# Softmax of the first two sub-blocks with one token per partition: dynamic convolution and squared-ReLU FFN

## The chip, the cores and the metric

The kernel runs on one core of a Trainium2 chip. The metric is device time in microseconds (us) of one execution; lower is better. The engines are PE (matmul, with its weight loads shown apart as PEld), DVE (vector), ACT (scalar), POOL (GpSimd) and SP (which here only issues DMAs). ACT and POOL can issue DMAs too.

## What is computed

The reference, cut to what matters (B=8, S=4096, D=192, 8 heads of 24 channels, K=7 taps, 2048 hidden columns):

```python
w = exp(weight_gen - max)                     # (B, S, 8 heads, 7 taps)
w = w / sum(w, axis=-1)                       # softmax over the taps
x_unf = x_pad[:, s + k, :]                    # 6 zeros ahead of x
out = einsum('bshk,bskhg->bshg', w, x_unf)    # a causal 7-tap conv, its weights differ by token and head
h = maximum(out.reshape(-1, 192) @ w_in, 0)   # w_in 192 x 2048
result = (h * h) @ w_out                      # w_out 2048 x 192
```

## The kernel before, in words

**Tiling.** The 32768 tokens are cut into 64 sub-blocks of 512 tokens (TB). The first two sub-blocks are blocks of their own, the others go in pairs; the FFN runs over blocks. For the conv a sub-block is cut into five row tiles (NT=5) of 128 tokens, placed 104 apart from 24 tokens before its start (`starts`), so that each tile holds the 6 tokens before the ones it yields. For every row tile the conv needs a banded matrix: row = input token, column = output token and head, value = the softmax weight of that tap.

**How the band is made.** A `Softmax` part covers 128*r tokens with r tokens per partition: load of the weights (`load`, L219), exp on ACT (L244), sum over the taps on DVE (L251), reciprocal (L258), and scaled products written along diagonals (L266) into a tile v, in which a token's row holds 8 shifted places for the weights. The rows must then get from "r tokens per partition" to "one token per partition in row tile i": the tile `wr`. For most parts this is a DMA (`wr_load`, or `wr_load_sbuf` at L361, which reads v in SBUF). For the first two sub-blocks it is done by PE: `select_rows` (L383) multiplies v by slices of a 0/1 matrix `sel`, 8 matmuls of 64 columns a row tile, and `copy_rows` (L391, ACT) brings the PSUM result to `wr`. `st_band` (L406, DVE) then multiplies `wr` by a band mask into `bd`.

**The conv and the FFN.** `st_conv_first` (L466) multiplies x in f16 by `bd`, 16 small matmuls a row tile, into PSUM; the result is copied to y (L476 on ACT and L477 on DVE for sub-block 0, L479 for sub-block 1). A unit of the FFN (`st_unit`) is a set of matmuls of y by w_in (L566 for the first two blocks, L581 later), Relu on ACT (L595) and a square on DVE (L599). The second matmul (L630) multiplies by w_out, and o_sb (L644, L646) collects the output.

**Order.** All instructions are written in a fixed order, engine by engine, by a plan string per block: `u` a unit, `B` bands, `C` the next conv, `E` an exp, `S` the rest of a softmax, `M` a second matmul, `L` a load. Engines run their instructions in that order; DMA queues are those of SP, POOL and ACT. The first FFN unit follows a written prologue:

- PE runs 46 matmuls on zeros (`spin`, L697).
- SP issues the loads of the first part s0 (14 rows a partition, in three pieces: 8 tokens and a halo of 6), x of sub-block 0 in f32 (`x_st`, L317 and L327), and half of w_in in f32 (`w_st`, L133 and L135).
- s0 has r=8, so it covers 1024 tokens: sub-blocks 0 and 1.
- POOL makes the band mask (L117, L120) and `sel` (L110), then waits for s0's reciprocal through a one-element copy (`gate`, L716), then issues x of sub-block 1, the other half of w_in (in f16, the DMA casts) and the weights of the next part s1. A second gate (L746) waits for `w_st`; then follow w_out (L183), s2's weights and x of sub-block 2.
- ACT casts x_st to f16 in three pieces (L342) between the copies of the selected rows: tile 0; copies of tiles 0 and 1; tiles 1 and 2 of x; copies of tiles 2 to 4; tiles 3 and 4 of x.
- ACT casts one half of w_st (columns of units 0 and 1; L740) ahead of the copy of y, DVE the other half (units 2 and 3) after it.

Of the kernel before, what the change touches and what calls it, by code (L numbers as in the profile page):

```python
# [9 lines left out]
def kernel(  # L10
# [26 lines left out]
    nc = tc.nc  # L37
    f32 = mybir.dt.float32
    f16 = mybir.dt.float16

    B, S, D = x.shape
# [3 lines left out]
    HK = H * KK  # L45
# [3 lines left out]
    HP = H // 2  # L49
# [47 lines left out]
    w_o = const.tile([P, NF, Dm], f16, name="w_o")  # L97
    mask = const.tile([P, P, 2], f16, name="mask")
    FIRST = 8
    NSEL = TB + TB - P + FIRST + P  # L100
    sel = const.tile([P, NSEL], f16, name="sel")
    PARTS = {0: (8, 8, 8, 8), 1: (8, 8, 16), 2: (16, 16)}
    v_big = const.tile([P, R + 2 * HALO, HP, SL, 2], f16, name="v_big")
    v_first = [
        const.tile([P, FIRST + 2 * HALO, HP, SL, 2], f16, name=f"v_first{i}") for i in (0, 1)
# [1 line left out]

    def row_select():

        nc.gpsimd.affine_select(  # L110
            out=sel, in_=sel, pattern=[[-1, NSEL]], compare_op=AluOp.not_equal,
            fill=1.0, base=FIRST - 1, channel_multiplier=FIRST,
        )

    def band_mask():
# [11 lines left out]


    x_st = {}

    def load_w_in(dst, q, eng):
        c = q * NQ
# [58 lines left out]
    class Softmax:  # L191
# [86 lines left out]
        def store(self, eng):  # L278
# [5 lines left out]
                in_=self.v[:, HALO : HALO + r].rearrange("p r g c e -> p (r g c e)"),  # L284
            )

    vd_t = {}

    def new_vd(b):
# [2 lines left out]
        return vd_t[b]  # L292


    x_t, wr_t, pr_t, bd_t, yp_t, y_t, g_t, gp_t, t1_t, o_t, o_sb_t = ({} for _ in range(11))

    def rows(ap2d, t0, width):

# [4 lines left out]

    def ends(b):
        rs = PARTS.get(b, (R,))
        return [P * sum(rs[: i + 1]) for i in range(len(rs))]

    def tile_start(j, i):

# [42 lines left out]
    def wr_load_sbuf(j, parts, order, engines):  # L352

        wr_t[j] = p_wr.tile([P, NT, HP, SL * 2], f16, name="wr")
        n = 0
        for i in order:
            t0 = max(j % NBB * TB + tile_start(j, i), 0)
            for s in parts:
                a, b = max(t0, s.t0), min(t0 + P, s.t0 + P * s.r)
                if a < b:  # L360
                    engines[n % len(engines)].dma_start(  # L361
                        out=wr_t[j][a - t0 : b - t0, i].rearrange("p g c -> p (g c)"),
                        in_=s.v[
                            (a - s.t0) // s.r : (b - s.t0) // s.r, HALO : HALO + s.r
                        ].rearrange("p r g c e -> p r (g c e)"),
                    )
                    n += 1

    def select_rows(j, s, tiles, places):

        if j not in wr_t:
            wr_t[j] = p_wr.tile([P, NT, HP, SL * 2], f16, name="wr")
        n = len(tiles) // len(places)
        for m, i in enumerate(tiles):
            if m % n == 0:
                pool, tag = places[m // n]
                prs = pool.tile([P, n, H * SL], f32, name="pr", tag=tag)
                pr_t[(j, i)] = prs
            pr = prs[:, m % n]
            a = max(j % NBB * TB + tile_start(j, i), 0) - s.t0  # L380
            for r in range(s.r):
                c = a + FIRST - 1 - r
                nc.tensor.matmul(  # L383
                    out=pr, lhsT=sel[:, c : c + P],
                    rhs=s.v[:, HALO + r].rearrange("p g c e -> p (g c e)"),
                    start=(r == 0), stop=(r == s.r - 1),
                )

    def copy_rows(j, tiles, n=1):
        for i in tiles[::n]:  # L390
            nc.scalar.copy(  # L391
                out=wr_t[j][:, i : i + n].rearrange("p t g c -> p t (g c)"),
                in_=pr_t.pop((j, i)),
            )

    def st_band(j, tiles):

# [48 lines left out]
    def st_conv_first(j):  # L446

        s = BLOCKS[j][0]
        y = p_y.tile([P, NK, TB], f16, name="y")
        y_t[j] = y  # L450
        if j == 0:
            yps = [ps_h.tile([P, TB], f32, name="yp", tag="h") for _ in range(2)]
        else:
            yp = ps_h.tile([P, 2, TB], f32, name="yp", tag="h")
            yps = [yp[:, k] for k in (0, 1)]
        places = [(q, 32 * q, 0) for q in range(4)]
        places += [(q, r0 + 32 * (q - 4), 1) for r0 in (0, RT) for q in (4, 5)]
        for i in ROW_ORDER:
            lo, b = bounds[i], bounds[i + 1]
            hi = lo + (STEP if tile_start(s, i) == starts[i] else b - lo)  # L460
            bd = bd_t[s][:, H * lo : H * hi].rearrange("p (g c e) -> p g e c", g=HP, e=2)
            for later in (True, False):
                for q, p0, k in places:
                    _, ha, hb, pre = quads[q]
                    m, h = (32, hb) if later else (pre, ha)
                    nc.tensor.matmul(  # L466
                        out=yps[k][p0 : p0 + m, lo:b],
                        lhsT=x_t[s][:, i, 32 * q : 32 * q + m],
                        rhs=bd[:, h // 2, h % 2, 0 : b - lo],
                        start=True,  # L470
                        stop=True,
                        skip_group_check=True,
                        tile_position=(0, p0),
                    )
        if j == 0:
            nc.scalar.copy(out=y[:, 0], in_=yps[0])  # L476
            nc.vector.tensor_copy(out=y[:, 1], in_=yps[1])  # L477
        else:
            nc.scalar.copy(out=y[:, 0:2], in_=yp)  # L479

    def st_conv_spread(j):

# [183 lines left out]
    with nc.allow_low_precision("fp16 matmul pipeline"), tc.manual_schedule():  # L666

        block_of = {n: j for j, (s, c) in enumerate(BLOCKS) for n in range(s, s + c)}
        parts = []
        for b in range(B):  # L670
            t0 = 0
            for r in PARTS.get(b, (R,)):
                v = v_first[len(parts) % 2] if r == FIRST else v_big
                parts.append(Softmax(b, t0, r, v, block_of[b * NBB + t0 // TB]))
                t0 += P * r
# [7 lines left out]
                wr_load_sbuf(j, near, range(NT), engines)  # L683

        warm = const.tile([P, TB], f16, name="warm")
        gate = const.tile([P, 1], f32, name="gate")
        nc.vector.memset(warm, 0.0)
        nc.vector.memset(sel, 0.0)
        for v in v_first:
            nc.vector.memset(v[:, HALO : HALO + FIRST], 0.0)  # L690

        WARM = 156
        wp = ps_o.tile([P, TB], f32, name="wp", tag="o0")
# [5 lines left out]
                    start=True, stop=True,  # L699
                )  # L700

        s0, s1, s2 = parts[:3]
        spin(46)
        band_mask()
        s0_cuts = (0, FIRST // 2, FIRST, s0.rh)
        s0.load(nc.sync, s0_cuts)
        w_st = p_wg.tile([P, (R + HALO) * HK], f32, name="w_st", tag="wg")[:, 0 : NQ + NQ // 2]
        x_load_f32(0)
        row_select()
        load_w_in(w_st, 0, nc.sync)  # L710
        for lo, hi in zip(s0_cuts, s0_cuts[1:]):
            s0.exp(lo, hi)
            s0.total(lo, hi)
            if hi >= FIRST:
                s0.recip(0 if hi == FIRST else FIRST, hi)
        nc.gpsimd.tensor_copy(out=gate, in_=s0.rcp[:, FIRST, 0, 0:1])  # L716
        x_load(1)
        load_w_in(w_i[:, 1, 0], 1, nc.gpsimd)
        s1.load(nc.gpsimd)
        s0.scale(0, s0.rh, nc.vector)  # L720
        x_cast(0, nc.scalar.copy, 0, 1)
        o0, o1, ring = (ps_o, "o0"), (ps_o, "o1"), (ps_h, "h")
        select_rows(0, s0, ROW_ORDER, (o1, ring, ring, ring, o0))
        copy_rows(0, ROW_ORDER[:2])
        x_cast(0, nc.scalar.copy, 1, 3)
        copy_rows(0, ROW_ORDER[2:])
        x_cast(0, nc.scalar.copy, 3, NT)
        for i in ROW_ORDER:
            st_band(0, (i,))
        select_rows(1, s0, ROW_ORDER, (o1,))  # L730
        copy_rows(1, ROW_ORDER, NT)

        def cast_w_in(e, copy):

            q = NQ // 4
            w0, w1 = (
                w.rearrange("p (a e c) -> p a e c", e=2, c=q)[:, :, e]
                for w in (w_st, w_i[:, 0, 0])
            )
            copy(out=w1, in_=w0)  # L740

        cast_w_in(0, nc.scalar.copy)
        st_conv_first(0)
        cast_w_in(1, nc.vector.tensor_copy)

        nc.gpsimd.tensor_copy(out=gate, in_=w_st[:, 0:1])  # L746
        for q in range(4):
            load_w_out(q, 4)
        s2.load(nc.gpsimd)
        x_load(2)  # L750
# [5 lines left out]
        steady = "MuMuuu" * 3 + "MuuuMCu"  # L756
        steady_spread = "MuMuuu" * 2 + "MuCMuuu" + "MuMuuu"
        plans = {
            0: "u B1 u u u E1 C S1 u u M u u",
            1: "L3 u u B2 M E2 B3 u u M E2 u S2 S2 u M u C u M",  # L760
            2: "L4 u u u E3 M u u u M B4 u u u u M B5 S3 u u u u M u C u",
            3: "L5 L6 u u E3 u M S3 u u u M u M E4 u u B6 u M u M B7 u u u E4 M u M C S4 u",
        }


# [23 lines left out]

        for n, s in enumerate(parts):  # L790
            k = n - min(m for m, p in enumerate(parts) if p.b == s.b)
            cuts = (0, s.rh) if n < 2 else CUTS_FOR.get((s.b, k), CUTS[s.r])
            s.pieces = list(zip(cuts, cuts[1:]))
            s.exps = iter(s.pieces)
            s.softs = iter(s.pieces)
        for n, s in enumerate(parts[4:], 4):
            b, f = s.b, s.fb
            k = n - min(m for m, p in enumerate(parts) if p.b == b)
            times = TIMES.get((b, k)) or (
# [156 lines left out]
```

## Time and profile before

| What | Value |
|---|---|
| runs | 729.57, 729.58, 731.94 us; median 729.58 us |
| the profiled execution: span from the first to the last instruction | 728.4 us |
| PE busy | 722.0 us (99%), 14078 matmuls |
| DVE busy | 625.8 us (86%) |
| ACT busy | 612.0 us (84%) |
| POOL busy | 98.5 us (14%) |
| granted TensorE clock | 1.000 |
| DMA | 68.30 MB, mean 94 GB/s |

The profiled execution's device time is not recorded apart from its span; what lies around the span is taken from the median of the runs, 729.58 - 728.4 = 1.2 us. The profile is of one execution. Its lines give, for an engine, a start and a length in us from the first instruction; "[0.80 <-DMA wg]" means that the engine had been idle for 0.80 us and that this load ended it. "L266" is line 266 of the kernel. "128x224 f32" is partitions by elements. The chain is followed back from the last instruction, at each step to what released it.

### The profile page before, as it was taken

To read this page: it belongs to the slowest core of one execution; us is meant where nothing else is said; L and a number is where in the kernel's file an instruction comes from. 1 tells how busy PE (TensorE), PEld (TensorE's weight loads), DVE (VectorE), ACT (ScalarE), POOL (GpSimd) and SP (SyncE) were. 2 spreads that over 40 slices of the span, in tenths; PEclk is the share of its full clock that TensorE was granted. 3 is DMA by queue.
4 is the path that set the end of the run, shared out by engine and by line. 5 is a ranking of instruction groups with operands and counts; after the bars stand their busy time and mean duration, and the time that the engine had idled before them with its cause. 6 is when DMAs were issued, how large, how long until landed. Compare 5 with 4: busy or idle time off the path is not lost.

```text
span 728.4 us, 31046 instructions
## 1 busy us (share of the span) xinstructions
PE 722.0 (99%) x14078; PEld 530.1 (73%) x14078; DVE 625.8 (86%) x839; ACT 612.0 (84%) x731; POOL 98.5 (14%) x146
## 2 busy tenths in 40 slices
PE   8999999999999999999999999999999999999998
PEld 5668877777777777777777777777777777777777
DVE  7999997998898998888988888988888988778753
ACT  6998888888888888888888888888888888888883
POOL 7231223411001100011001010010000110001000
PEclk9999999999999999999999999999999999999999
DMA  9664465676245443356432554343544325444112
GB/s 193 128 113 106 82 125 89 128 142 138 78 71 133 99 84 68 75 116 125 83 62 58 135 104 88 66 74 110 114 78 87 57 53 117 67 87 77 30 46 67
DMA packets 126272, 68.30 MB, mean 94 GB/s; under 512 B 85353, under 2 KB 122556, under 8 KB 125628
## 3 DMA queue, kind: packets, MB, share of 16 engines
q0 software_dynamic: 46192, 19.43, 22.9%
q1 hardware_dynamic: 79804, 46.79, 22.5%
q8 instruction: 110, 1.80, 1.1%
q14 instruction: 22, 0.18, 0.1%
q10 hardware_dynamic: 144, 0.10, 0.0%
HBM read 50.18 MB, written 28.70 MB: 108 GB/s over the span
## 4 chain that ended last, share of the span: by engine, by line
PE 98%; DMA 1%; SPq 0%; ACT 0%; issue 0%; ACTq 0%
PE o L630 47%; PE h L581 44%; PE yp L502 4%; PE h L566 2%; PE yp L536 1%; DMA w_st<-in_moe_w_in_dram 1%; SPq L219 0%; PE yp L466 0%; ACT w_i L740 0%; SPq L135 0%; SPq L133 0%; ACT y L476 0%; SPq L327 0%; SPq L317 0%; ACT o_sb L644 0%
## 5 line engine op out<-in xcount | busy, mean ns | idle before, releaser
L595 ACT ACTIVATE t<-h 128x1024 f16<-128x1024 f32 x512 | 496.6, 1027 | 60.1 <-PE h L581 58.4
L630 PEld LDWEIGHTS <-g 64*128 64x128 f16 (+1 forms) x8032 | 344.3, 94 | 55.2 <-issue 2.3
L630 PE MATMUL o<-w_o,g 64*128 64x192 f16 (+1 forms) x8032 | 380.1, 243 | 0.1
L599 DVE TENSOR_TENSOR g<-t 128x2048 f16<-128x2048 f16 (+1 forms) x287 | 307.4, 1105 | 28.7 <-ACT t L595 28.3
L581 PE MATMUL h<-y,w_p 64*128 64x512 f16 x2400 | 291.7, 376 | 0.0
L581 PEld LDWEIGHTS <-w_p 64*128 64x128 f16 x2400 | 113.9, 94 | 94.8
L406 DVE TENSOR_TENSOR bd<-wr,mask 128x4160 f16<-128x4160 f16 (+4 forms) x90 | 149.5, 1685 | 1.2 <-ACT wr L391 1.2
L646 DVE TENSOR_TENSOR o_sb<-o,o_sb 128x384 f32<-128x384 f32 x123 | 68.4, 556 | 61.4 <-ACT o_sb L644 60.3
L327 POOL DMA_DIRECT2D xt<-in_x_dram x63 | 52.6, 838 | 415.4 <-PE yp L502 362.5
L644 ACT COPY o_sb<-o 128x384 f32<-128x384 f32 x129 | 61.6, 477 | 45.7 <-PE o L630 44.4
L581 PE MATMUL h<-y,w_i 64*128 64x512 f16 x576 | 70.5, 376 | 0.0
L581 PEld LDWEIGHTS <-w_i 64*128 64x128 f16 x576 | 30.5, 94 | 21.7 <-issue 1.2
L502 PEld LDWEIGHTS <-xt 128*32 128x32 f16 x2000 | 24.6, 95 | 10.6 <-issue 10.6
L266 DVE TENSOR_TENSOR v_big<-ex,rcp 128x112 f16<-128x112 f32 (+5 forms) x180 | 29.9, 237 | 2.1 <-DMA vd<-v_big 1.1
L512 DVE CAST y<-yp 128x1024 f16<-128x1024 f32 x25 | 30.4, 1218 | 0.0
L502 PE MATMUL yp<-bd,xt 128*32 128x104 f16 (+1 forms) x2000 | 28.4, 210 | 0.0
L244 ACT ACTIVATE ex<-wg 128x560 f32<-128x560 f32 (+5 forms) x40 | 26.3, 659 | 1.2 <-DMA wg<-in_weight_gen_dram 1.2
L251 DVE TENSOR_REDUCE ssum<-ex 128x80 f32<-128x560 f32 (+5 forms) x40 | 25.6, 639 | 1.3 <-ACT ex L244 1.3
L512 ACT CAST y<-yp 128x1024 f16<-128x1024 f32 x25 | 25.2, 1007 | 0.0
L258 DVE RECIPROCAL rcp<-ssum 128x64 f32<-128x64 f32 (+4 forms) x39 | 23.0, 589 | 1.4
L317 POOL DMA_DIRECT2D xt<-in_x_dram x7 | 3.9, 555 | 120.4 <-PE yp L502 109.4
L361 POOL DMA_DIRECT2D wr<-v_first x24 | 13.0, 559 | 24.0 <-DVE v_first L266 23.8
(42 smaller groups left out, 111.9 us busy)
## 6 DMA issues: line engine op xcount, KB each, us to landing
out_dram<-o_sb SPq DMA_DIRECT2D x63, 384.0 KB
xt<-in_x_dram POOLq DMA_DIRECT2D x42, 240.0 KB, 4.9
wg<-in_weight_gen_dram SPq DMA_DIRECT2D x4, 1064.0 KB
xt<-in_x_dram POOLq DMA_DIRECT2D x21, 192.0 KB, 5.0
wr<-vd SPq DMA_DIRECT2D x38, 80.0 KB
vd<-v_big SPq DMA_DIRECT2D x5, 512.0 KB
y<-y SPq DMA_DIRECT2D x100, 24.0 KB
wg<-in_weight_gen_dram SPq DMA_DIRECT2D x3, 616.0 KB
```

The lines of the kernel that those rows point to most:

```text
L244: nc.scalar.activation(out=self.ex[:, lo:hi].rearrange("p r g k e -> p (r g) k e"), in_=self.wg[:, lo:hi].rearrange("p r (g e) k -> p (r g ...
L266: eng.tensor_tensor(out=bass.AP(tensor=v.tensor, offset=v.offset + lo * H * SL + lo % SL * 2 + g * SL * 2, ap=[list(v.ap[0]), [H * SL + 2, ...
L327: eng.dma_start(out=dst[:, first:last], in_=ap)
L406: nc.vector.tensor_tensor(out=bd_t[j][:, H * lo : H * (lo + len(tiles) * n)].rearrange("p (g m c) -> p g m c", g=shape[1], c=2 * SL), in0= ...
L502: nc.tensor.matmul(out=yp[p0 : p0 + 32, k - k0, a:b], lhsT=x_t[s][:, i, c0 : c0 + 32], rhs=bd[:, head // 2, e, 0 : b - a], start=True, sto ...
L512: copy(out=y[:, k0 : k0 + 2], in_=yp)
L581: nc.tensor.matmul(out=h[:, half], lhsT=w_in_chunk(w, u, slot, half), rhs=y_t[j][r0 : r0 + RT, k], start=(slot == 0), stop=(slot == NK - 1 ...
L595: nc.scalar.activation(out=t1[:, e], in_=h, func=ActF.Relu)
L599: nc.vector.tensor_tensor(out=g[:, a : e + 1], in0=t1[:, a : e + 1], in1=t1[:, a : e + 1], op=AluOp.mult)
L630: nc.tensor.matmul(out=oo[:, cc * Dm : (cc + 1) * Dm], lhsT=g[r0 : r0 + n, cc * P : (cc + 1) * P], rhs=w_o[r0 : r0 + n, fc, :], start=(fc ...
L644: nc.scalar.copy(out=o_sb, in_=o[0][:, c])
L646: nc.vector.tensor_tensor(out=o_sb, in0=o[1][:, c], in1=o_sb, op=AluOp.add)
```

## The change

The softmax of sub-blocks 0 and 1 no longer goes through a `Softmax` part and `select_rows`. A new class `Head`, one per sub-block, loads the weights of each row tile with one token per partition (five tiles, 56 values each), so that exp, sum, reciprocal and one product are done for all five tiles at once, without shifting. The shift comes in `select`: for each of the 8 places c and 7 taps k, one matmul multiplies by a shifted identity, a slice of `sel`, and adds up over the taps in PSUM; 56 matmuls of 40 columns for a sub-block, for all its row tiles together.

Around it: the spin has 36 matmuls instead of 46; the first head's tiles 1 to 4 are loaded through ACT's queue, tile 0 and the second head through SP's; w_in's first half is split by units, so that units 0 and 1 are loaded by POOL in f16 and units 2 and 3 by SP in f32 into `w_st` and cast by ACT after y; both gates go; w_out's first two quarters are issued ahead of the next part's weights. On ACT the copies of head 0 come ahead of all three x casts, the copy of head 1 after them. The PSUM result of conv 0 is split by row tiles (the first three, the last two) instead of by channels, and copied in three pieces. The remaining parts of batch 0 are three, from token 1024 on; the 6 rows ahead of sub-block 2's first own token come from the halo rows of that part (a POOL memset and a small DMA), and sub-block 1's last row tile is no longer moved to its end. In the plans, the parts are renumbered.

```diff
-    PARTS = {0: (8, 8, 8, 8), 1: (8, 8, 16), 2: (16, 16)}
+    NHEAD = 2
+    WSEL = P + SL
+    sel = const.tile([P, SL, WSEL], f16, name="sel")
+    PARTS = {0: (8, 8, 8), 1: (8, 8, 16), 2: (16, 16)}
...
+    def load_w_in_set(dst, e, eng):
+        n = NQ // 4
+        w = moe_w_in[:, 0:NQ].rearrange("d (a e c) -> d a e c", e=2, c=n)
+        eng.dma_start(out=dst[:, 0:2], in_=w[0:P, :, e])
+        for a in (0, 1):
+            eng.dma_start(out=dst[RT * a : RT * (a + 1), 2], in_=w[P:D, a, e])
...
+    class Head:
...
+        def load(self, *engines):
+            w = weight_gen[0].rearrange("s h k -> s (h k)")
+            t0 = self.j * TB
+            a = int(t0 == 0)
+            if a:
+                engines[1].dma_start(out=self.wg[:, 0], in_=w[0:P, :])
+            ap = rows(w, t0 + starts[a], HK)
+            engines[0].dma_start(
...
+        def exp(self):
+            nc.scalar.activation(
+                out=self.ex.rearrange("p t (g k e) -> p (t g) k e", k=KK, e=2),
+                in_=self.wg.rearrange("p t (g e k) -> p (t g) k e", e=2, k=KK),
+                func=ActF.Exp,
+            )
...
+        def scale(self):
+            ex = self.ex.rearrange("p t (g k e) -> p (t g) k e", k=KK, e=2)
+            nc.vector.tensor_reduce(
+                out=self.ssum, in_=ex.rearrange("p g k e -> p g e k"), axis=AxisX, op=AluOp.add,
+            )
+            nc.vector.reciprocal(out=self.rcp, in_=self.ssum)
+            nc.vector.tensor_tensor(
+                out=self.ws.rearrange("p t g k e -> p (t g) k e"), in0=ex,
+                in1=self.rcp.unsqueeze(2).broadcast_to((P, NT * HP, KK, 2)),
+                op=AluOp.mult,
+            )
...
+        def select(self, pool, tag):
+            wr_t[self.j] = p_wr.tile([P, NT, HP, SL * 2], f16, name="wr")
+            self.pr = pool.tile([P, NT, HP, SL, 2], f32, name="pr", tag=tag)
+            for c in range(SL):
+                for k in range(KK):
+                    d = KK - 1 - k
+                    nc.tensor.matmul(
+                        out=self.pr[:, :, :, c, :], lhsT=sel[:, c, d : d + P],
+                        rhs=self.ws[:, :, :, k, :], start=(k == 0), stop=(k == KK - 1),
+                    )
...
+        if j == NHEAD:
+            r0, r1 = -BASE - HALO, -BASE
+            nc.gpsimd.memset(wr_t[j][0:32, 0], 0.0)
+            engines[1].dma_start(
...
+        c = bounds[split]
+        nc.scalar.copy(out=y[:, 0:2, 0:c], in_=yps[0][:, :, 0:c])
+        if c < TB:
+            nc.scalar.copy(out=y[:, 0, c:], in_=yps[1][:, 0, c:])
+            nc.vector.tensor_copy(out=y[:, 1, c:], in_=yps[1][:, 1, c:])
...
-        spin(46)
+        spin(36)
         band_mask()
...
-        nc.gpsimd.tensor_copy(out=gate, in_=s0.rcp[:, FIRST, 0, 0:1])
...
+        row_select()
+        h0.load(nc.scalar, nc.sync)
+        h1.load(nc.sync)
+        x_load_f32(0)
...
+        load_w_in_set(w_i0[:, :, 0], 0, nc.gpsimd)
+        load_w_in_set(w_st, 1, nc.sync)
         x_load(1)
         load_w_in(w_i[:, 1, 0], 1, nc.gpsimd)
+        h0.exp()
+        h1.exp()
+        h0.scale()
+        h1.scale()
+        h0.select(ps_o, "o1")
+        h1.select(ps_o, "o0")
+        h0.copy(0, 1)
+        h0.copy(1, NT)
+        for lo, hi in ((0, 1), (1, 3), (3, NT)):
+            x_cast(0, nc.scalar.copy, lo, hi)
         for i in ROW_ORDER:
             st_band(0, (i,))
+        h1.copy(0, NT)
         st_conv_first(0)
+        nc.scalar.copy(out=w_i0[:, :, 1], in_=w_st)
...
-        nc.gpsimd.tensor_copy(out=gate, in_=w_st[:, 0:1])
-        for q in range(4):
+        for q in (0, 1):
+            load_w_out(q, 4)
+        s1.load(nc.gpsimd)
+        for q in (2, 3):
             load_w_out(q, 4)
         s2.load(nc.gpsimd)
```

## The prediction

> **What bounds the kernel now.** I read the shares first (part 1 of the page), then the chain that ended last (part 4), then the same chain in order of time for the first 40 us, then the timeline of the first 13 us. PE is busy 722.0 us of a span of 728.4 us, and the whole chain is PE:
>
> ```profile
> PE 98%; DMA 1%; SPq 0%; ACT 0%; issue 0%; ACTq 0%
> ```
>
> The chain in order of time (start, length, what) shows where PE becomes dense:
>
> ```profile
> 4.33 6.39 DMA w_st<-in_moe_w_in_dram
> ...
> 10.83 0.83 ACT w_i L740
> 11.66 0.49 ACT y L476
> 12.15 0.04 issue
> 12.20 3.17 PE h L566 x16
> 15.37 1.06 PE yp L466 x66
> ```
>
> From 12.20 us on, PE does not wait again: its list of waits has three entries, 1.3, 1.0 and 0.7 us, all before 12.20. So what the change is worth is almost exactly how far it moves the first FFN matmul (L566), and at most a few us are there. The chain names the load of w_st, but that is a near tie. The timeline (start, length, engine, line) shows the second arm, softmax to conv:
>
> ```profile
> 0.81 1.28 ACT L244 ACT_TABLE_LOAD   x1 [0.81 <-PEq L940]
> ...
> 2.89 0.41 ACT L244 ACTIVATE ex<-wg 128x224 f32<-128x224 f32 x1 [0.80 <-DMA wg<-in_weight_gen_dram]
> ...
> 7.21 2.44 PE L383 MATMUL pr<-v_first,sel 128*128 128x64 f16 x78 [0.41 <-DVE v_first L266]
> ...
> 7.58 0.45 ACT L391 CAST wr<-pr 128x64 f16<-128x64 f32 x2 [2.68 <-PE pr L383]
> 7.90 1.09 DVE L406 TENSOR_TENSOR bd<-wr,mask 128x832 f16<-128x832 f16 x2 [0.75 <-ACT wr L391]
> ...
> 8.81 0.51 ACT L342 CAST xt<-x_st 128x384 f16<-128x384 f32 x1 [0.78 <-DMA x_st<-in_x_dram]
> ...
> 9.47 1.60 DVE L406 TENSOR_TENSOR bd<-wr,mask 128x832 f16<-128x832 f16 x3 [0.47 <-ACT wr L391]
> ...
> 11.56 0.58 ACT L476 CAST y<-yp 128x512 f16<-128x512 f32 x1
> ```
>
> The five band products (L406) end at 11.07, the conv at 11.47, y at 12.14, the FFN starts at 12.20. Two things hold the bands: they start at 7.90, and the last three wait 0.47 us because the copies of their rows stand on ACT behind the cast that waits for x (8.81).
>
> **What the change removes.** The x cast now stands behind the copies of sub-block 0's rows, so the bands no longer wait for x. The 128x768 cast of w_i ahead of the FFN (0.83 us at 10.83) goes: that half is loaded as f16 by POOL, and the other half of w_st is half as large and is cast after y. The gates (L716 held POOL 2.86 us, L746 0.36 us) go, so POOL issues from about 2.35 us (mask ends at 2.06, the new sel select has 128 columns where 256 took 0.39 us) instead of 6.14.
>
> **What it puts in their place, on the path.** One detail decides. ACT's first instruction is now a DMA issue, and exp of the first head waits for two DMAs. The order of the built instructions shows one of these waits on the exp itself and the other as an instruction of its own *ahead of the table load*. Before, the table load had no wait and ran at 0.81, under the flight of the DMA. So its 1.28 us come after the landing.
>
> The landing is not in the trace. The head's 640 packets of 224 B have the bytes of one of the old first loads (140 KB against 112 KB), which was there at 2.89: lower end 2.9. If each packet cost as much as the old ones (the second and third load, 128 packets each, were there at 3.58 and 4.15, so 0.63 us per 128), 512 more make 2.89+2.5 = 5.4: upper end. The nearest row in packet size is the later load of 128 B rows:
>
> ```profile
> q1 hardware_dynamic: 1047, 0.13, 86.2%
> ```
>
> That is the queue's packets, MB and share in the stretch 127 to 128 us: 1047 small packets in 1 us, so 512 more are 0.5 us, less the part that overlaps. I take 3.3.
>
> The sum, with 0.05 us for each handover between engines (exp ends 3.30, reduce starts 3.33; y ends 12.14, PE starts 12.20):
> - landing 3.30, handover, table load 1.28: 4.63.
> - exp of 280 columns, 0.46 (224 took 0.41, 336 took 0.51): 5.09.
> - handover, reduce of 280 to 40, 0.42 (224: 0.39, 336: 0.45), reciprocal of 40, 0.40 (48: 0.45, 64: 0.55), one product of 280, 0.39 (the 84 and 112 column ones take 0.24 and 0.26): 6.35.
> - handover, 56 selects: spacing (2.44-0.19)/77 = 0.029 us from L383, and 0.19 for the last: 1.79, so 8.19. All five tiles are ready together.
> - handover, ACT copy of tile 0, 64 columns, 0.21: 8.45.
> - handover, five bands of 0.53 (1.09 for two, 1.60 for three), no wait between: 2.67, so 11.17, where before it was 11.07.
> - last conv tile, 0.40 as before (11.07 to 11.47): 11.57.
> - ACT copy of the last 200 columns of y: 0.07 and 0.34 (64 take 0.21, 320 take 0.45): 11.98. DVE's copy of the second part waits for ACT's, 0.37 more, but the FFN's first two matmuls need only the first part and take 0.43 us.
> - handover: the first FFN matmul at **12.03 against 12.20, so 0.2 us earlier**.
>
> **What lies beside it, and its cover.**
> - Second head: 56 more selects end at 9.8; conv tile 2 waits for its band until 10.05 anyway. 0.
> - x: ACT reaches the first large cast at about 9.2. x was there at 8.78, though issued 0.5 us later than now; POOL's earlier traffic may slow it. ACT then needs 0.51, 0.53, 0.45 (second head's rows) and 0.70 for the first 312x2 columns of y: 11.4, ahead of the last copy at 11.64. Cover 0.2 us; beyond that each us costs one.
> - w_i's first half: issued by POOL from 2.35 to 4.1; the same tile's loads took 5.5 us (median) to land, so 9.6, due at 12.0. The longest such load of POOL took 8.0: 12.1.
> - w_st: due on ACT at 12.0, was there at 10.7 with twice the bytes. Its cast (0.83) stands ahead of the first Relu, which would wait for PE until 12.9 anyway (1.0 us of such a wait at 13.15 before). 0.
> - POOL, with eight loads in flight at most: the next part's weights (wg) are issued at about 8.5, were issued at 9.17, now behind two loads of w_o; landing in 5.6 to 7.7 us makes 14 to 16.2, due at 16.6 (exp at 16.78). 0, above 16.6 one for one. w_o lands by 15, due at 17.7.
> - PE's warm spin is 10 shorter and ends near 5.2; the pause until 6.4 is 1.2 us, against pauses of 0.6 and 0.4 before. No row shows the rate after such a pause; at half rate the first selects would cost 1.6 us more, at the rate of L383 nothing. I take nothing.
> - The halo memset and DMA of sub-block 2 replace a piece of the same kind on the same queues, 0. From block 0 on, the plan of units is the same.
>
> [...] The trace has the table load at 1.28 us and 0.80 us between its end and the exp, ended by a DMA; so anything that follows a load is at most 0.80 us here. [...]
>
> **Time.** The profiled execution spans 728.4 us; the runs' median is 729.58, 1.2 us over it, which I leave as it is. 729.58-0.2 gives **729.4**. The likeliest case's own range is 0.6 us to either side.
>
> **Rivals.**
> 1. *Small packets bind (slower than before).* The 1280 packets of 224 B for the heads cost by number, not bytes; the first head lands at 5.4, all that follows moves by 2.1: 14.1, time 731.5. For: the early loads took 0.63 us per 128 packets. Against: the 1047 packets in one us. It decides from a landing of 3.5 on; from there the kernel is slower than before.
> 2. *The table load hides after all* (the chip has it before the landing). Bands end 1.3 us earlier, and x on ACT becomes the bound: cast from 8.8, y copied by 11.25, FFN at 11.3, 0.9 earlier: 728.7; with x at 7 us 10.75, 728.1. Against: the wait stands ahead of the load.
> 3. *A transfer binds*: w_i by POOL at 12.1 or more, or x 1 us late, because POOL's loads run beside SP's from the start. FFN at 12.2 to 13.0: 729.6 to 730.4. For: the DMA share was already over 0.8 in most us from 2 to 8.
>
> **Chances.** Forecast 0.55, rival 1 0.17, rival 2 0.13, rival 3 0.12, anything else 0.03. The range 728.0 to 731.5 takes in rivals 2 and 3 and the upper end of the landing, and leaves out less than 2 in 10. A difference of 0.5% is 3.6 us, about what a measurement of this kernel can tell from no change; every priced case is inside it. Faster 0.02, same 0.94, slower 0.04 (a landing beyond 5.4 together with a late transfer).
>
> **What would show it.** In the profile after: the table load starting after 3 us and not at 0.81; exp near 4.6; select from 6.4 to 8.2; no gap between the bands; the last at 11.2; L620 (the FFN) at 12.0. Wrong if the table load is at 0.8 to 1.3, if PE's selects space at over 0.045 us, if L620 waits for a DMA, or if PE waits again after its first unit.

## The result, and the profile after

The changed kernel takes **733.15 us** (median of 9 runs, 731.77 to 735.40) against 730.16 us for the kernel before beside it (9 runs, 729.17 to 731.94). The ratio is 1.0046, interval 1.0032 to 1.0060: 3.0 us slower, where the prediction said 729.4 and a range of 728.0 to 731.5. The profiled execution is the one of 731.77 us, the lowest of the nine.

The page of the kernel after: the span (728.4 before), the instructions of each engine, a queue that comes up below, and the shares of the chain.

```profile
span 730.1 us, 31075 instructions
...
PE 723.7 (99%) x14100; PEld 532.5 (73%) x14100; DVE 624.2 (86%) x830; ACT 611.7 (84%) x728; POOL 98.8 (14%) x147
...
q8 instruction: 110, 1.80, 1.1%
...
PE 96%; DVE 1%; DMA 1%; ACT 1%; issue 0%; DVEq 0%; ACTq 0%
```

PE is still the whole chain. Its order in time (start, length, what) is the view to set beside the one of before:

```profile
0.81 1.92 DMA wg_head<-in_weight_gen_dram
...
2.81 1.28 ACT L326
...
4.10 0.47 ACT ex_head L326
...
5.51 0.46 DVE ws_head L338
...
6.02 4.57 PE pr L350 x112
10.59 1.12 PE yp L520 x69
11.71 1.45 issue
13.16 0.26 PE yp L520 x4
...
13.45 0.33 ACT y L532
...
13.83 3.18 PE h L620 x16
17.00 1.07 PE yp L520 x66
```

The FFN (L620) starts at 13.83, where it started at 12.20: 1.63 us later, and the span is 1.7 us longer. So nearly all of this execution's loss lies ahead of 13.83, and one line of the chain is nearly as long as the loss: 1.45 us of "issue" at 11.71, in the middle of the conv of sub-block 0. "Issue" means that the profile shows nothing that PE waited for. PE's list of waits (total, times, longest) says the same:

```profile
PE yp L520 <- issue: 1.5, 1, 1.5
...
PE h L620 <- ACT y L532: 0.4, 1, 0.4
```

The timeline gives the place to one matmul:

```profile
8.42 0.49 ACT L356 CAST wr<-pr 128x64 f16<-128x64 f32 x2 [3.51 <-PE pr L350]
...
8.74 2.60 DVE L461 TENSOR_TENSOR bd<-wr,mask 128x832 f16<-128x832 f16 x5 [1.50 <-ACT wr L356]
...
10.52 1.20 PE L520 MATMUL yp<-bd,xt 128*32 128x104 f16 x75
...
13.16 0.25 PE L520 MATMUL yp<-bd,xt 128*24 128x96 f16 x5 [1.45 <-issue]
```

The last band (L461) is done at 11.34, so PE had its data from then on. It stops with 75 of the conv's 80 matmuls done. Counted from the start of PE's program that is 36 of the spin, 112 selects and 75: the pause stands ahead of the **224th matmul**. Ahead of the FFN the new program has 36+112+80 = 228 matmuls, the old one 46+80+80 = 206.

What moved beside it: in the stretch 10.9 to 11.1 us the DMA view (packets, MB, share) has one packet on the queue that the page names "instruction", of 0.02 MB. The page counts 110 such packets, 1.80 MB in all, or 16 KB each. PE's 14100 matmuls and as many weight loads are 256 to a packet; no other engine has more than 830 instructions. That this queue brings PE its program is the author's inference from its name and these counts; no line of the profile shows it.

```profile
q8 instruction: 1, 0.02, 29.6%
```

It starts at 10.91 in the trace, takes 0.95 us, and PE goes on 2.25 us after its start.

**The second part of the loss** is not in this execution. The granted clock was 0.999 or more in four of the nine runs, at 731.8 to 732.5 us (their middle 731.9, 1.75 over the kernel before, about what the FFN's start explains), and 0.995 to 0.998 in the other five, at 733.15 to 735.4. The kernel before shows 0.999 or more in all 56 runs beside the experiments.

### The profile page after: what moved, and what is told of

Its sections match the earlier page's. It is cut to its first block, busy times and chain, and to the rows that moved or that the text cites. A ratio compares the mean times of both kernels' runs of the same rounds, so it can differ in the third digit from the quotient of the medians.

```text
span 730.1 us, 31075 instructions
## 1 busy us (share of the span) xinstructions
PE 723.7 (99%) x14100; PEld 532.5 (73%) x14100; DVE 624.2 (86%) x830; ACT 611.7 (84%) x728; POOL 98.8 (14%) x147
## 4 chain that ended last, share of the span: by engine, by line
PE 96%; DVE 1%; DMA 1%; ACT 1%; issue 0%; DVEq 0%; ACTq 0%
PE o L684 46%; PE h L635 43%; PE yp L556 4%; PE h L620 2%; PE yp L590 1%; DMA vd<-v_big 1%; PE pr L350 1%; DVE g L653 0%; PE yp L520 0%; DMA wg_head<-in_weight_gen_dram 0%; ACT t L649 0%; DVE v_big L278 0%; ACT L326 0%; DVE o_sb L700 0%; ACT ex_head L326 0%
## 5 line engine op out<-in xcount | busy, mean ns | idle before, releaser
L461 DVE TENSOR_TENSOR bd<-wr,mask 128x4160 f16<-128x4160 f16 (+4 forms) x89 | 149.4, 1704 | 1.5 <-ACT wr L356 1.5
L256 ACT ACTIVATE ex<-wg 128x560 f32<-128x560 f32 (+4 forms) x37 | 25.0, 677 | 0.0
L263 DVE TENSOR_REDUCE ssum<-ex 128x80 f32<-128x560 f32 (+4 forms) x37 | 24.3, 658 | 0.0
L270 DVE RECIPROCAL rcp<-ssum 128x80 f32<-128x80 f32 (+4 forms) x37 | 22.0, 594 | 1.3
```

The costliest lines, as they stand in the source:

```text
L256: nc.scalar.activation(out=self.ex[:, lo:hi].rearrange("p r g k e -> p (r g) k e"), in_=self.wg[:, lo:hi].rearrange("p r (g e) k -> p (r g ...
L461: nc.vector.tensor_tensor(out=bd_t[j][:, H * lo : H * (lo + len(tiles) * n)].rearrange("p (g m c) -> p g m c", g=shape[1], c=2 * SL), in0= ...
```

## The experiments

**Theory** (fetch, a guess from the place of the pause and the packet beside it). PE waits for its next instructions at a fixed matmul of its program, so what counts is how many matmuls stand ahead of the FFN, not what they work on. **Rivals:** the narrow selects are at fault (they space at 0.039 us, where 0.029 was expected), the later table load is, or the shorter spin (36 for 46) is, through the clock.

### Fewer, wider spin matmuls (e1_spin_wide)

25 matmuls fewer ahead of the conv, with as many columns in all, and nothing else:

```diff
-        WARM = 156
+        WARM = 512
...
-        spin(36)
+        spin(11)
```

> The changed kernel with the warm spin of 11 matmuls of 512 columns (5632 columns) in place of 36 of 156 (5616): the same length of PE work, 25 matmuls fewer in PE's program. Theory fetch: the pause of 1.45 us that PE makes in the last conv tile, put down to no releaser, is the wait for a block of PE's program that is reached too early; with 25 matmuls fewer it is reached only in the FFN, the pause goes, the FFN starts at 12.4 instead of 13.83, the time falls by 1.4 us against the changed kernel (to 731.7 of a median of 733.15). Theory data: the pause is a wait for x or a band; it stays, and the time stays. Theory clock: the spread of the changed kernel's runs (731.8 to 735.4) goes with the mean granted clock (1.000 to 0.995), and since the spin is as long, the spread stays as it was.

Measured: 730.72 us (11 runs, 729.82 to 731.82), ratio to before 1.0010 (1.0001 to 1.0019), clock 0.999 or more in every run. The timeline of PE:

```profile
10.39 1.24 PE L520 MATMUL yp<-bd,xt 128*32 128x104 f16 x80
12.15 3.17 PE L620 MATMUL h<-y,w_i 128*128 128x512 f16 x16 [0.52 <-ACT y L532]
```

All 80 matmuls of the conv stand in one group, and the FFN starts at 12.15 (the prediction's sum was 12.03). Of the 3.0 us over the kernel before, 0.7 are left (730.00 beside it): 25 matmuls on zeros fewer take 2.3 us away. That is more than the 1.4 us expected, because the clock is not lost either (0.995 to 0.998 in five of the changed kernel's nine runs), although the spin is as long as it was (4.66 us for 4.65): the expectation that the spread would stay was wrong. The selects, the table load and the order of the loads are those of the changed kernel, so none of these makes the pause by what it does; the selects count by their number. The 224th matmul now lies in the conv behind the first FFN matmuls, and PE's list of waits shows nothing there.

### The table load early (e2_table_early)

The changed kernel, with a one-column exp that needs no transfer placed right behind the first loads:

```diff
         h0.load(nc.scalar, nc.sync)
+        early = const.tile([P, 1], f32, name="early")
+        nc.scalar.activation(out=early, in_=warm[:, 0:1], func=ActF.Exp)
```

> The changed kernel with one exp of a single column of the zero tile on ACT directly behind its DMA issue, which waits for nothing but a memset, so that the table load stands ahead of the wait for the weights. Theory table: the load's 1.28 us leave the path, the first head's exp starts at 2.9 instead of 4.10, the selects start 1.2 us earlier if the warm spin is over by then (it ends at 5.1 to 5.9, the products would be ready at 4.8), so 0.1 to 0.9 us earlier at the selects; the time falls by as much, or by less where the casts of x bind. Theory hidden: the load costs nothing on the path, and the time stays within 0.3 us.

Measured: 733.34 us (6 runs, 732.51 to 735.27), ratio 1.0048 (1.0036 to 1.0061): no gain. The edit does what it says on ACT; the load runs under the flight of the DMA and exp starts 0.7 us earlier (3.41 for 4.10):

```profile
1.29 1.28 ACT L763 ACT_TABLE_LOAD   x1 [1.29 <-PEq L986]
...
3.41 0.46 ACT L326 ACTIVATE ex_head<-wg_head 128x280 f32<-128x280 f32 x1 [0.63 <-DMA wg_head<-in_weight_gen_dram]
```

PE's timeline tells where the 0.7 us went:

```profile
9.82 1.19 PE L520 MATMUL yp<-bd,xt 128*32 128x104 f16 x75
12.93 0.25 PE L520 MATMUL yp<-bd,xt 128*24 128x96 f16 x5 [1.92 <-issue]
13.59 4.72 PE L620 MATMUL h<-y,w_i 128*128 128x512 f16 x16 [0.41 <-ACT y L532]
```

The same 75 and 5. PE comes to the pause 0.70 earlier (11.01 for 11.71) and leaves it 0.23 earlier, so the pause grows from 1.45 to 1.92: its end is set by something other than PE. The 16 KB packet starts at 10.73 in this trace, 2.20 us ahead of that end.

The first 16 FFN matmuls take 4.72 us, not 3.18. The table by stretches (length, busy time of PE, PEld, DVE, ACT and POOL with counts, granted clock, DMA share, GB/s) shows the clock, which is the number right behind POOL's bracket:

```profile
12.00:14.00 2.00, 0.66 (x7) 0.28 (x6) 0.43 (x2) 0.79 (x2) 0.97 (x3) 1.00 1.37 221
14.00:16.00 2.00, 2.00 (x9) 0.54 (x8) 2.00 (x1) 1.57 (x3) 2.00 (x2) 0.65 1.37 240
16.00:18.00 2.00, 2.00 (x8) 0.27 (x6) 1.39 (x2) 1.62 (x2) 1.04 (x1) 0.50 1.40 283
18.00:20.00 2.00, 2.00 (x86) 1.19 (x86) 0.60 (x2) 1.80 (x3) 0.32 (x1) 1.00 0.83 127
```

0.65 over 14 to 16 is full clock for 0.6 us and half for 1.4: the clock is at half from 14.6 to 18.0, 3.4 us, while PE is fully busy.

### The selects' output in one stretch (e3_out_flat)

PSUM is laid out so that a select writes 40 adjacent columns; the copies read it permuted:

```diff
-            self.pr = pool.tile([P, NT, HP, SL, 2], f32, name="pr", tag=tag)
+            self.pr = pool.tile([P, SL, NT * HP, 2], f32, name="pr", tag=tag)
...
-                        out=self.pr[:, :, :, c, :], lhsT=sel[:, c, d : d + P],
+                        out=self.pr[:, c], lhsT=sel[:, c, d : d + P],
...
```

> The changed kernel with the selects' PSUM tile laid out by place first, so that each select writes 40 columns in a row instead of 20 pairs 16 columns apart; ACT's copies read it permuted. Theory stride of the output: the selects' spacing falls from 0.040 us to 0.025 to 0.029 us, both heads' selects end 1.2 to 1.6 us earlier (4.57 us down to about 3.2), the bands start 0.6 us earlier, the time falls by 0.6 to 1.5 us. Theory operand or load: the spacing stays 0.040 us and the time stays. Theory clock: if the clock falls because the narrow selects keep PE too little busy, faster selects do not cure that, and the spread of the runs stays.

Measured: 734.2 us (6 runs, 731.41 to 734.92), ratio 1.0045 (1.0029 to 1.0061). The row of the selects (ns min/median/max, first and last start) is nearly that of the changed kernel, which is shown with f1_wide_rhs_flat below:

```profile
L350 PE MATMUL pr<-ws_head,sel x112: 196/211/213, 6.1 to 10.5; 128*128 128x40 f16 x112
```

Their spacing does not move (0.039 us), so the output's stride is not its cause. The pause stands at the same matmul; the packet starts at 11.25 in the trace, 2.45 ahead of its end:

```profile
13.70 0.32 PE L520 MATMUL yp<-bd,xt 128*24 128x96 f16 x5 [1.90 <-issue]
```

The clock falls here for twice as long, in the same kind of table:

```profile
12.00:14.00 2.00, 0.30 (x5) 0.15 (x5) 0.00 (x0) 0.08 (x1) 0.55 (x1) 0.87 1.48 241
14.00:16.00 2.00, 1.59 (x7) 0.29 (x6) 1.59 (x2) 1.06 (x2) 1.45 (x2) 0.50 1.39 240
16.00:18.00 2.00, 2.00 (x6) 0.43 (x4) 1.01 (x1) 1.61 (x2) 1.88 (x1) 0.50 1.33 295
18.00:20.00 2.00, 2.00 (x7) 0.27 (x6) 1.23 (x1) 1.45 (x2) 0.00 (x0) 0.50 0.83 104
20.00:22.00 2.00, 2.00 (x87) 1.28 (x86) 0.75 (x1) 1.80 (x3) 0.39 (x1) 0.92 0.00 0
```

0.87 and 0.92 at the ends give half clock from 13.5 to 20.3, 6.8 us. From 14 to 18 us PE was 90% busy, at half speed.

### The old kernel with the shorter spin (e4_before_spin36)

```diff
-        spin(46)
+        spin(36)
```

> The kernel before with 36 spin matmuls in place of 46, that part of the change alone. Theory spin: the shorter spin makes PE's clock rise later in some executions or fall again, so the median rises by 1 to 1.5 us, the mean granted clock falls below 0.999 in some runs and the spread grows to over 3 us. Theory selects: the clock is lost by the 112 narrow selects, not by the spin; then this kernel stays within 0.5 us of the kernel before, at a clock of 1.000 in most runs.

Measured: 730.24 us (11 runs, 729.46 to 731.64), ratio 1.0003 (0.9995 to 1.0012). In its chain the FFN starts no later than in the kernel before, and PE's list of waits has no "issue":

```profile
11.79 3.17 PE h L566 x16
```

The shorter spin costs nothing by itself that these runs can tell, so this rival falls as the cause of the loss. One of the eleven runs (730.83 us) shows a clock of 0.998, the others 1.000; what that one comes from is not shown.

### The old kernel with 22 matmuls more (f4_before_plus22)

The counterpart of the first experiment: the old selects and loads, but 228 matmuls ahead of the FFN. The spin's matmuls are narrower, so that it ends nearly as before (6.20 us for 5.96).

```diff
-        WARM = 156
+        WARM = 106
...
-        spin(46)
+        spin(68)
```

> The kernel before with a spin of 68 matmuls of 106 columns in place of 46 of 156: the same columns, 22 matmuls more in PE's program, so that as many stand ahead of the FFN as in the changed kernel (228). Theory fetch: PE pauses ahead of its 224th matmul, as the changed kernel, e2 and e3 did, here in the last conv tile, with no releaser; the pause is 0.5 to 1.7 us, the time rises by as much, and where the clock falls after it, by up to 3 us more. Theory selects: the pause belongs to the new selects or loads; there is none here, and the time stays at that of before.

Measured: 731.1 us (11 runs, 729.79 to 734.17), ratio 1.0017 (1.0005 to 1.0028). PE's timeline:

```profile
9.45 1.30 PE L466 MATMUL yp<-bd,xt 128*32 128x104 f16 x75
11.27 0.25 PE L466 MATMUL yp<-bd,xt 128*24 128x96 f16 x5 [0.52 <-issue]
12.15 1.13 PE L566 MATMUL h<-y,w_i 128*128 128x512 f16 x6 [0.63 <-ACT y L476]
```

68+80+75 = 223 again: the pause came with the number, without one line of the change. The packet (the only one of its queue from 8 to 11 us) starts at 8.95 in the trace, 2.32 ahead of its end. Here the pause is 0.52 us long and lies mostly under the cast of w_i that holds ACT until 11.35, so the FFN starts at 12.15 and the profiled span is 728.7. This run shows that the pause exists, not what it costs. The rest of the ratio is in other executions: three of the eleven show a clock of 0.997 to 0.998 (732.16, 733.00 and 734.17 us); the middle of the other eight is 730.4.

### Wider spin and the selects' input in one stretch (f1_wide_rhs_flat)

A select reads 20 pairs of numbers, 14 numbers apart. Here the weights are laid out tap first, so that it reads 40 adjacent ones; the spin is the wide one:

```diff
-            self.ws = const.tile([P, NT, HP, KK, 2], f16, name=f"ws_head{j}")
+            self.ws = const.tile([P, KK, NT * HP, 2], f16, name=f"ws_head{j}")
...
-                        rhs=self.ws[:, :, :, k, :], start=(k == 0), stop=(k == KK - 1),
+                        rhs=self.ws[:, k].rearrange("p (t g) e -> p t g e", g=HP), start=(k == 0), stop=(k == KK - 1),
...
```

> The kernel of e1 (spin of 11 wide matmuls), and the selects' moving operand laid out tap first, so that each select reads 40 numbers in a row instead of 20 pairs 14 numbers apart; DVE's product writes it permuted. In e1 the selects stand 0.0393 us apart, and e3 showed that the order of the output doesn't matter. Theory operand: spacing falls to 0.025 to 0.029 us, the first head's selects end 0.6 to 0.8 us earlier, the bands move with them, the FFN starts at 11.4 instead of 12.15, the time falls by 0.6 to 0.8 us against e1 (730.72), so to about that of before. Theory weights: the spacing is that of the 128-column weight loads; it stays, and so does the time.

Measured: 729.42 us (11 runs, 728.94 to 730.47), ratio to before 0.9994 (0.9985 to 1.0003). The selects by tile (ns min/median/max, first and last start), first of the changed kernel:

```profile
L350 PE MATMUL pr<-ws_head,sel x112: 197/211/215, 6.0 to 10.4; 128*128 128x40 f16 x112
```

and then of this one:

```profile
L350 PE MATMUL pr<-ws_head,sel x112: 179/179/180, 6.1 to 8.9; 128*128 128x40 f16 x112
```

112 take 2.98 us instead of 4.57: 0.025 us apart instead of 0.039. The input's stride is the cause. The output is written here as in the changed kernel, in pairs 16 columns apart. Of 1.6 us less on PE the FFN's start gains 0.69 over the first experiment (11.46 for 12.15), because the bands on DVE hold the conv now. The chain:

```profile
8.03 2.61 DVE bd L461 x5
...
10.68 0.38 PE yp L520 x16
...
11.46 3.17 PE h L620 x16
...
29.38 1.55 PE yp L590 x110
```

### Wider spin and the early table load (f2_wide_table), and all three (f3_wide_table_rhs)

The first is the early exp with `WARM = 512` and `spin(9)`; the second adds the tap-first layout.

> The kernel of e2 (table loaded ahead of the wait) with a spin of 9 matmuls of 512 columns, which ends at about 5.1 at the low rate, and 27 matmuls fewer in PE's program, so no pause in the conv. Theory fetch: in e2 the end of the pause, not the work, set the FFN's start, which hid the earlier table; without the pause the 0.6 us by which exp moves (3.41 against 3.97 to 4.10) reach the FFN: it starts at 11.5, the time is 0.5 to 0.7 us under e1. Theory x: the casts of x or the load of w_i bind at about 11.3 to 12, and less than 0.3 us is left of it.

> Both repairs of f1 and f2 and the wide spin of 9. If all that was found adds up, the first select starts at 5.3, ends at 6.8, the bands end at 9.7, the FFN starts at 10.5 to 10.8, 1.4 us before that of the kernel before, and the time is 729.0 to 729.3 against 730.0 of before. If a transfer binds (w_i by POOL landed late, x), the FFN starts at 11 to 11.5 and waits for a DMA, and the time is that of before.

Measured: 729.38 us (11 runs, 729.03 to 730.54), ratio 0.9990 (0.9981 to 0.9999), FFN at 11.38; and 729.81 us (11 runs, 728.64 to 730.48), ratio 0.9996 (0.9987 to 1.0004), FFN at 10.95. The lines of PE's timelines, first of the one, then of the other:

```profile
11.38 3.18 PE L620 MATMUL h<-y,w_i 128*128 128x512 f16 x16 [0.52 <-ACT y L532]
```

```profile
10.95 3.17 PE L620 MATMUL h<-y,w_i 128*128 128x512 f16 x16 [0.42 <-ACT y L532]
```

With no pause behind it the early table load is worth what it saves on ACT: 0.77 us of FFN start over the first experiment (12.15 to 11.38). It is the only version whose interval lies below the kernel before, by 0.1% and barely, as that of the first experiment lies barely above it.

The version with all three missed what was expected of it (FFN at 10.5 to 10.8, 729.0 to 729.3 us). Part of that is ahead of the FFN: the first head's selects take 1.88 us here and 1.58 in f1, as the two chains show, first this one:

```profile
5.29 1.88 PE pr L350 x56
```

and then f1:

```profile
6.11 1.58 PE pr L350 x56
```

The second head's selects end 1.44 and 1.40 us after them (all 112 take 3.49 us from 5.12 here, 2.98 from 6.11 in f1), so the difference is in the first ones. PE is slower in its first microseconds in the traces of before and after too: the spin's matmuls of 156 columns start 0.130 us apart up to 4.25 and 5.55 us, and 0.067 from there. That the first selects fell into such a stretch here is the author's estimate from these spacings.

Its earlier FFN is then given back. The conv of block 2 (L590) starts in the chain at

```profile
29.25 1.53 PE yp L590 x106
```

29.25 us, against 29.38 and 29.30 in the other two: of 0.43 to 0.51 us gained at the FFN's start 0.05 to 0.13 is left. Its list of PE's waits has one that the other two do not have:

```profile
PE o L684 <- DVE o_sb L700: 0.7, 1, 0.7
```

and ACT waits there for the next part's weights (0.27 us at 15.95, ended by their DMA). What was on time behind an FFN at 12.2 looks to be late behind one at 10.95; no run moved these loads.

## Why the prediction was wrong, step by step

The prediction's chain against the profile of after, in us:

| step | predicted | measured |
|---|---|---|
| first head lands | 3.30 | 2.81 |
| table load ends | 4.63 | 4.09 |
| exp ends | 5.09 | 4.57 |
| product ends | 6.35 | 5.97 |
| selects of the first head, copy of tile 0 ends | 8.45 | 8.63 |
| bands end | 11.17 | 11.34 |
| conv ends | **11.57** | **13.42** |
| y, then the FFN starts | 12.03 | 13.83 |

- **The step that failed** is "last conv tile, 0.40 as before (11.07 to 11.47): 11.57". From the bands' end the conv took 2.08 us, of which 1.45 is the pause ahead of the 224th matmul. The prediction counted the new matmuls by their time (56 selects more "end at 9.8; conv tile 2 waits for its band until 10.05 anyway. 0") and never as instructions of PE's program. Two experiments show that their number decides: 25 fewer take the pause away, 22 more bring it to the old kernel.
- **Second, "I take nothing" for the clock after a pause.** The prediction weighed half rate for a pause of 1.2 us ahead of the selects. That pause did not come: the spin ended at 5.91 us and not "near 5.2", 0.1 us ahead of the first select. The clock was lost with the other pause, which was not foreseen. Half clock for 3.4 us (e2) is at most 1.7 us lost, for 6.8 us (e3) 3.4: added to the 731.9 of the undisturbed runs this gives 733.6 and 735.3 (estimates), and the runs at 0.998 and 0.995 lie at 733.85 and at 735.16 and 735.40; the two at 0.997, 733.15 and 734.33, lie about and between.
- **The table load** stands behind the landing and costs 1.28 us there, as the order of the instructions said. Rival 2 is out. Exp starts at 4.10, 0.01 us behind the load's end at 4.09, so nothing more of the load stood on the path.
- **The landing** was 0.5 us better than taken: the first head's 640 packets of 224 B were there at 2.81 and not at 5.4, rival 1 is out.
- **The selects** cost more than "0.029 us" each: 0.039, 2.4 us for the first 56 and not 1.79. That took back the 0.4 us which the landing and the products had left, and 0.2 more. The row used for the price, L383, reads 64 columns; nothing of the stride was weighed.
- **Transfers** (rival 3): the FFN waited for y on ACT (0.4 us), not for a DMA. The covers given for x, w_i and w_st held.
- **The rest of the sum came out, partly by luck:** the landing was 0.5 us better than taken and the selects 0.6 worse. Without the pause the FFN starts at 12.15 (first experiment), 0.05 ahead of before and 0.12 behind the forecast; the time is then 730.72 against 730.00 beside it, 0.7 us slower, though its profiled span (728.1) is no longer than that of before. What these 0.7 us are is open; the profiled execution is the second fastest of the eleven (729.87 us), so its FFN's start need not be that of the others. In f1 and f2 the FFN starts 0.74 and 0.82 us ahead of before, and the time is 0.72 and 0.76 us below the kernel before beside them. So the change itself, without the pause, brings no gain: the interval, 1.0001 to 1.0019, lies just above 1.
- **Its own signs.** "Wrong if ... PE waits again after its first unit" did not name the place: the new pause is ahead of the FFN.

## What to carry to other kernels

Matmuls added ahead of a tuned start-up can cost more than their own time: here 22 more brought a pause of 1.45 us (0.52 in f4). Count PE's matmuls from its start to the first long ones, look for an "issue" entry in PE's list of waits, and if there is one, try warm-up matmuls that are fewer and wider (11 of 512 columns for 36 of 156 took 2.3 us off here). Price a pause of PE just ahead of its dense part with more than one run, and with the clock: here some executions with the pause ran at half clock for 3.4 or 6.8 us. Once the pause is gone, an earlier start can be given back further on (the version with all three kept 0.05 to 0.13 us of 0.4 to 0.5).

## What the runs showed of the hardware that had not been expected

- **PE stops at a place of its program.** In four kernels (after, its two variants with the narrow spin, the old one with 22 matmuls more) it stood still for 1.45, 1.92, 1.90 and 0.52 us, always ahead of the 224th matmul, and went on 2.25, 2.20, 2.45 and 2.32 us after a 16 KB packet of an "instruction" queue had started. In the other six kernels the 224th matmul came due 2.71 to 5.22 us after the start of that packet, and none of them paused. That PE waited for this packet is inferred from the queue's name and size, the place and these distances; the trace names no releaser. What sets the packet's start is open: PE had begun 135 to 216 matmuls by then. Why PE goes on only 2.2 to 2.5 us after it, when the packet itself takes 0.95 to 0.99 us in these four, and whether POOL's transfers of that time (55 packets beside it in 0.2 us) slow it, was not tried.
- **The place alone does not cost the pause.** In the kernel before the 224th matmul came at 15.30 us, 5.22 after that packet's start at 10.08, and PE did not stop there; in the changed kernel the 223 ahead of it were done by 11.71, 0.80 after the packet's start, and 1.45 us showed.
- **The clock halved for longer than the pause beside it.** With pauses of 1.92 us (e2) and 1.90 (e3) it was 0.50 for 3.4 us in one execution and for 6.8 in the other. Without a pause of this kind the mean was 0.999 or more in all 44 runs of the first experiment and f1 to f3, and in all 56 of the kernel before, which has the narrow spin, and in ten of the eleven of e4; with one it was 0.995 to 0.998 in 5 of 9, 4 of 6, 4 of 6 and 3 of 11.
- **What decides whether the clock falls is not shown.** In e2 it fell at 14.6 us, 1.7 after the pause had ended; in e3 at 13.5, 0.2 before the end. In the 3.4 us ahead of the drop PE was busy for 0.37 (e2) and 0.50 (e3) of the time. In the profiled execution of after it was busy for 0.45 of the 3.41 us from 10.42 to 13.83, and the clock stayed at 1.00. So neither the pause nor PE's busy share over such a stretch settles it.
- **A moving operand of 20 pairs 14 numbers apart** made a matmul of 40 columns take 0.039 us (after) instead of 0.025 (f1) back to back; with an output in PSUM of pairs 16 columns apart 0.025 was reached (f1), and one of 40 adjacent columns left 0.039 as it was (e3).
